# One ring of three PSUM banks for transposed scores and value product

## The chip, the cores and the metric

The kernel runs on one core of a Trainium2 chip. Its engines work side by side, each on its own queue in program order: TensorE (PE, with its weight loads shown apart as PEld), VectorE (DVE), ScalarE (ACT), GpSimd (POOL), and SyncE (SP), which issues the DMAs. They wait for each other through semaphores. TensorE writes its products to PSUM, which has eight banks of 128 partitions by 512 fp32 values; ScalarE and VectorE read them from there. The metric is the device time of one execution in microseconds, the median of several runs.

## The reference

Four layers in a row on a sequence of 2048 positions by 640 channels: attention, Fourier mixing, attention, Fourier mixing, each with a layer norm ahead and its input added behind.

```python
def _A_ref(x, wqkv, wo):                      # H = 32 heads of Dh = 20, window W = 256
    qkv = (x @ wqkv).reshape(B, S, 3, H, Dh).transpose(2, 0, 3, 1, 4)
    q, k, v = qkv[0], qkv[1], qkv[2]
    scores = jnp.einsum("bhqd,bhkd->bhqk", q, k) * (Dh ** -0.5)
    mask = (idx[:, None] - idx[None, :] >= 0) & (idx[:, None] - idx[None, :] < W)
    p = _softmax(jnp.where(mask[None, None], scores, -1e9), axis=-1)
    o = jnp.einsum("bhqk,bhkd->bhqd", p, v)
    return o.transpose(0, 2, 1, 3).reshape(B, S, D) @ wo
def _B_ref(x, ...):                            # y = Cr @ (x Wr^T) - Ci @ (x Wi^T)
x = x + _A_ref(_layernorm(x), A_wqkv, A_wo)
x = x + _B_ref(_layernorm(x), ...)             # and both once more
```

Only the two attention layers are touched by the change.

## The kernel before

An attention layer treats its 32 heads as eight quads of four, and the 2048 positions as 16 blocks of 128. The function `heads` walks through 8 x 16 = 128 steps, preceded by ten lead steps; one step is one quad and one block. Because of the window of 256, a block of queries sees at most three blocks of keys. In this document the steps of a layer are counted from 0 to 127, as the variable `t` does.

Every step does the same work for three places of the sequence at once:

- **Scores for the maximum** (`s_head`, line 553), ten steps ahead: queries by keys for one head, into the banks 2, 3 and 4 in turn. VectorE adds the mask and takes each row's maximum (line 558). Every fourth step `m_rows` transposes the maxima on TensorE (line 565), ScalarE copies them negated (line 567), and a DMA of SP puts them as an extra row under the queries (line 569).
- **Transposed scores** (`t_head`, line 578): keys by queries for one head, with that extra row, so that the maximum is already subtracted. ScalarE takes the exponential into SBUF (`t_exp`, line 587), and POOL clears what the mask excludes (`t_mask`, lines 593 and 597). The four heads of a quad are two halves `z` of two heads `e`; the text calls their transposed scores T00 and T01 (z = 0) and T10 and T11 (z = 1). Head `e` uses bank `e`: bank 0 for T00 and T10, bank 1 for T01 and T11.
- **Value product** (`pv`, line 608), one step behind: up to three blocks of keys, each as four matmuls on four column tiles of TensorE, which give one block of the output, 128 columns. A column of ones among the values gives the sum of the exponentials beside it. Bank 5 holds four such blocks side by side. After every second block ScalarE copies two of them, 256 columns, to the tile `ou` in SBUF (line 617); there are two such tiles in turn. After four blocks `finish` sends a tile out by two DMAs (lines 628 and 629), and ScalarE may write it again once these have landed.

Between the halves z = 0 and z = 1 of a step, `fill` puts other matmuls on TensorE: first the query and key projections of later quads (line 191, through banks 6 and 7), which come in rounds of 8, 8, 8 and 6 a step, and, when those are done (after step 91), the output projection. A finished projection is copied out by ScalarE (line 477), split on POOL and stored. Weights for it are split on ScalarE (line 160) and POOL (line 166).

The order on each engine is the order in which this Python code issues the instructions; no scheduler moves anything. A matmul into a bank waits for the engine that read the bank's former contents. Such a wait stops all of TensorE's later matmuls, though a weight load may run while an earlier matmul streams. The order inside one step is set by these lines:

```python
            for z in range(2):
                for e in range(2):
                    heads = [(t_head, t, e), (s_head, s, 1 - e)]
                    ...
                if 0 <= t < steps:
                    for e in range(2):
                        t_exp(t // 16, t % 16, z, e, e + 1)
                    ...
                if z:
                    relieve()
                    if 0 <= v < steps:
                        pv(v // 16, v % 16)
```

Of the kernel before, what the change touches and what calls it, by code (L numbers as in the profile page):

```python
# [11 lines left out]
AF = mybir.ActivationFunctionType  # L12
# [5 lines left out]
P = 128  # L18
# [45 lines left out]
class Net:  # L64
# [457 lines left out]
    def heads(self, xsrc, xdst, hook):  # L522
        nc = self.nc
        qp = [t.rearrange("p (z s) -> p z s", z=2) for t in self.qp]
        kp = [t.rearrange("p (z s) -> p z s", z=2) for t in self.kp]
# [4 lines left out]
        def defer(d, fn):  # L530
            later.setdefault(now[0] + d, []).append(fn)
# [3 lines left out]
        def load_v(n):  # L535
            if n < 4 * NQ:
                nc.sync.dma_start(self.vq[n % 3][:, :384].rearrange("p (t c) -> p t c", c=96),
                                  self.vd[n // 4][:, n % 4 * 4:n % 4 * 4 + 4, :])

        mc = {}  # L540
        turn = [0]

        def s_bank():
            turn[0] += 1
# [17 lines left out]
        def m_rows(quad, u):  # L562
            m = mc.pop((quad, u))
            p = self.banks[:16, s_bank(), :P]
            nc.tensor.transpose(p, m.rearrange("p z e j -> p (z e j)"), self.ident)  # L565
            mt = pool.tile([16, P], F32R, name="mt", tag="mt", bufs=1)
            nc.scalar.activation(mt, p, AF.Copy, scale=-1.0)
            for z in range(2):
                self.post(1, lambda z=z: nc.sync.dma_start(
                    qp[quad % 2][60:125:64, z, u * 512:(u + 1) * 512].bitcast(F32),  # L570
                    mt[8 * z:8 * z + 8, :].bitcast(F32)))

        pt = {}

        def t_head(quad, kb, z, e):
            n = min(NB - kb, 3)
            b = 64 * e
            nc.tensor.matmul(  # L578
                self.banks[:, e, :n * P], kp[quad % 2][b:b + 61, z, kb * P:(kb + 1) * P],
                qp[quad % 2][b:b + 61, z, kb * P:(kb + n) * P], start=True, stop=True)  # L580

        def t_exp(quad, kb, z, e0, e1):
            n = min(NB - kb, 3)
            if z + e0 == 0:
                i = 0 if (quad, kb) == (NQ - 1, NB - 1) else kb % 4
                pt[quad, kb] = self.pt[i].rearrange("p (h s) -> p h s", h=4)
            nc.scalar.activation(pt[quad, kb][:, 2 * z + e0:2 * z + e1, :n * P], self.banks[:, e0:e1, :n * P],  # L587
                                 AF.Exp, scale=SCALE)

        def t_mask(quad, kb, z):  # L590
            n = min(NB - kb, 3)
            t = pt[quad, kb][:, 2 * z:2 * z + 2, :]
            nc.gpsimd.affine_select(  # L593
                out=t[:, :, 0:P], in_=t[:, :, 0:P], pattern=[[0, 2], [1, P]],
                compare_op=OP.is_ge, fill=0.0, base=0, channel_multiplier=-1)
            if n == 3:
                nc.gpsimd.affine_select(  # L597
                    out=t[:, :, 256:384], in_=t[:, :, 256:384], pattern=[[0, 2], [-1, P]],
                    compare_op=OP.is_gt, fill=0.0, base=0, channel_multiplier=1)

        def pv(quad, qb):

            p = self.banks[:, 5, qb % 4 * P:qb % 4 * P + P]
            for kb in range(max(qb - 2, 0), qb + 1):
                t = pt[quad, kb]
                vq = self.vq[(4 * quad + kb // 4) % 3]
                for h in range(4):
                    nc.tensor.matmul(  # L608
                        p[32 * h:32 * h + 32, :], vq[:, 96 * (kb % 4) + 21 * h:96 * (kb % 4) + 21 * h + 32],
                        t[:, h, (qb - kb) * P:(qb - kb + 1) * P], start=kb == max(qb - 2, 0), stop=kb == qb,  # L610
                        tile_position=(0, 32 * h), skip_group_check=True)
            pt.pop((quad, qb - 2), None)
            if qb % 4 == 0:
                now_ou[0] = self.next("ou")
            if qb % 2:
                cs = slice(qb % 4 * P - P, qb % 4 * P + P)
                nc.scalar.activation(now_ou[0][:, cs], self.banks[:, 5, cs], AF.Copy)
            if qb % 4 == 3:
                finish(quad, qb // 4, now_ou[0])

        now_ou = [None]

        def finish(quad, bk, ou):
            sm = pool.tile([P, 16], F32, name="sm", tag="sm")
            rc = pool.tile([P, 16], F32, name="rc", tag="rc")
            cols = slice(bk * 512, (bk + 1) * 512)
            at = (2, 12, 14) if quad < NQ - 1 else (1, 5, 6)
            self.post(at[0], lambda: nc.sync.dma_start(sm, ou[0:P:32, :]))
            self.post(at[0], lambda: nc.sync.dma_start(
                self.od[4 * quad:4 * quad + 4, :, cols].rearrange("h r s -> (h r) s"), ou))  # L630
            self.post(at[1], lambda: nc.vector.reciprocal(out=rc, in_=sm))

            def store():
                nc.sync.dma_start(
                    self.rd[bk, 4 * quad:4 * quad + 4, :].rearrange("h (a b) -> (h a) b", b=16), rc)
                self.stored.add((quad, bk))
            self.post(at[2], store)
# [15 lines left out]
        def relieve():  # L653
            while self.heavy:
                self.relieve()
# [15 lines left out]
        def fill(n):  # L671

            k, size = 0, 1
            while k < size:
                r = more()
                if r == 0 and k == 0:
                    continue
                if r != 1:
                    return
                k += 1  # L680
                if k == 1:
                    left = self.left + 1
                    size = -(-left // max(1, round(left / n)))
            if self.left == 0:
                more()
                if self.heavy:
                    self.relieve()
# [4 lines left out]
        for step in range(-LEAD, steps + 1):  # L692
            now[0] = step
            self.wide, self.lead, self.tiled = step + LEAD > steps, step < -2, step < steps - 1
            for f in later.pop(step, []):
                f()
            s, t, v = step + LEAD, step, step - 1
            if due and s >= due[0][0]:
                while done[0] < due[0][1]:
                    fill(15)  # L700
                due.pop(0)
                q, j = (s + AHEAD) // 16, (s + AHEAD) % 16 // 4
                for i, f in enumerate(self.pack(q, j)):
                    defer(i // 3, f)
                for f in later.pop(step, []):
                    f()
            if v >= 0 and v % 4 == 3:
                load_v(v // 4 + 2)
            if done[0] < total:
                nf = max([FIRST if t < 0 else RATE]  # L710
                         + [(d - done[0]) / max(1, at - s) for at, d in due])
            elif made[0] < early:
                nf = LATE
            else:
                nf = LATE
            rows = ((s - 1) // 16, ((s - 1) % 16) // 4) if 4 <= s < steps + 4 and s % 4 == 0 else None
# [3 lines that stand above are left out]
                    for head, n, i in heads[::-1] if e else heads:  # L720
                        if 0 <= n < steps:
                            head(n // 16, n % 16, z, i)
                if 0 <= t < steps:
                    for e in range(2):
                        t_exp(t // 16, t % 16, z, e, e + 1)
                    t_mask(t // 16, t % 16, z)
                if z:
                    relieve()
                    if 0 <= v < steps:
                        pv(v // 16, v % 16)  # L730
                    if rows:
                        m_rows(*rows)
                if z == 0 and t >= 0 or t < -1 or t >= steps:
                    fill(nf)
                self.tick()
            if step > 16 * (NQ - 1):
                self.poll_late(step - 16 * (NQ - 1))
# [989 lines left out]
```

## Time and profile before

| what | value |
|---|---|
| median of 3 runs | 2180.93 us (2180.86 to 2181.6) |
| the profiled execution's own time | 2180.11 us |
| its span in the trace | 2178.4 us |
| line 578, transposed scores, x1024 | 310.6 us busy, mean 370 ns |
| line 587, exponentials, x1024 | 430.5 us busy, mean 470 ns |
| line 608, value product, x5760 | 214.9 us busy, mean 278 ns |
| line 553, scores for the maximum, x1024 | 280.2 us busy, mean 360 ns |
| line 191, filling projections, 512 columns, x1920 | 269.6 us busy, mean 394 ns |
| line 558, mask and maximum on VectorE, x1024 | 526.8 us busy, mean 558 ns |

Busy times of one line are unions, so overlapping matmuls count once; the mean is that of one instruction. The 128 steps of the first attention layer start at 161.1 us of the span, those of the second at 1242.6 us. In a row of a timeline stand the start, the length of a run of like instructions, the engine, the line, the operation, its tiles and shapes, and their count; in brackets the idle time ahead and what ended it. A matmul of TensorE is one row on PE and its weight load one on PEld.

### The profile page before, as it was taken

To read this page: it belongs to the slowest core of one execution; us is meant where nothing else is said; L and a number is where in the kernel's file an instruction comes from. 1 tells how busy PE (TensorE), PEld (TensorE's weight loads), DVE (VectorE), ACT (ScalarE), POOL (GpSimd) and SP (SyncE) were. 2 spreads that over 40 slices of the span, in tenths; PEclk is the share of its full clock that TensorE was granted. 3 is DMA by queue.
4 is the path that set the end of the run, shared out by engine and by line. 5 is a ranking of instruction groups with operands and counts; after the bars stand their busy time and mean duration, and the time that the engine had idled before them with its cause. 6 is when DMAs were issued, how large, how long until landed. Compare 5 with 4: busy or idle time off the path is not lost.

```text
span 2178.4 us, 49193 instructions
## 1 busy us (share of the span) xinstructions
PE 2123.0 (97%) x17893; PEld 1777.4 (82%) x17893; DVE 1615.0 (74%) x3933; ACT 1150.3 (53%) x2483; POOL 930.8 (43%) x1458
## 2 busy tenths in 40 slices
PE   7999999899999999999999999998999999999999
PEld 7987777687878888889999877776877788888899
DVE  6348788786897868777751578886868878687777
ACT  3117777766554545543431277776665545455522
POOL 3037777875514223230130477777754333331300
PEclk9999999999999999999999999999999999999999
DMA  5546666786435454657646466667753454546653
GB/s 184 176 154 189 202 183 213 219 221 212 134 119 175 138 185 129 216 192 264 218 135 190 152 200 185 201 203 219 226 188 134 131 187 137 164 148 217 219 175 126
DMA packets 221618, 395.40 MB, mean 182 GB/s; under 512 B 39360, under 2 KB 85952, under 8 KB 221376
## 3 DMA queue, kind: packets, MB, share of 16 engines
q1 hardware_dynamic: 221376, 392.26, 57.0%
q8 instruction: 141, 2.31, 0.5%
q14 instruction: 101, 0.83, 0.1%
HBM read 273.94 MB, written 117.05 MB: 179 GB/s over the span
## 4 chain that ended last, share of the span: by engine, by line
PE 81%; DVE 6%; POOL 5%; ACT 4%; issue 2%; DMA 2%; SPq 0%; ACTq 0%; DVEq 0%; POOLq 0%
PE banks L1266 27%; PE banks L173 14%; PE banks L191 13%; PE banks L608 8%; PE banks L578 6%; PE banks L1521 6%; PE banks L553 4%; POOL big L166 1%; POOL ou L1196 1%; DVE qp L166 1%; ACT big L928 1%; PE banks L273 1%; DVE pt L1197 1%; POOL rs L978 1%; PE banks L565 1%
## 5 line engine op out<-in xcount | busy, mean ns | idle before, releaser
L558 DVE CUSTOM_DVE_ANT_0 banks<-banks,mask 128x384 f32<-128x384 f32 (+2 forms) x1024 | 526.8, 558 | 157.9 <-PE banks L553 119.3
L587 ACT ACTIVATE pt<-banks 128x384 f32<-128x384 f32 (+2 forms) x1024 | 430.5, 470 | 179.3 <-PE banks L553 95.4
L578 PE MATMUL banks<-qp,kp 61*128 61x384 f32 (+2 forms) x1024 | 310.6, 370 | 14.5 <-DMA qp<-mt 7.8
L593 POOL TENSOR_SCALAR_AFFINE_SELECT pt<-pt 128x256 f32<-128x256 f32 x512 | 212.8, 416 | 183.5 <-ACT pt L587 133.2
L553 PE MATMUL banks<-kp,qp 60*128 60x384 f32 (+2 forms) x1024 | 280.2, 360 | 1.4 <-DVE mc L558 1.1
L191 PE MATMUL banks<-big,wc 64*128 64x512 f32 x1920 | 269.6, 394 | 0.4 <-DVE pt L374 0.4
L578 PEld LDWEIGHTS banks<-qp,kp 61*128 61x128 f32 x1024 | 175.2, 185 | 79.9 <-ACT pt L587 35.3
L608 PE MATMUL banks<-pt,vq 128*32 128x128 f32 x5760 | 214.9, 278 | 2.9 <-POOL pt L593 2.9
L191 PEld LDWEIGHTS banks<-big,wc 64*128 64x128 f32 x1920 | 183.0, 185 | 28.0 <-ACT x L477 5.2
L608 PEld LDWEIGHTS banks<-pt,vq 128*32 128x32 f32 x5760 | 144.0, 109 | 57.5 <-issue 51.5
L597 POOL TENSOR_SCALAR_AFFINE_SELECT pt<-pt 128x256 f32<-128x256 f32 x448 | 186.5, 416 | 0.0
L1196 POOL TENSOR_TENSOR pt<-pt,pt 128x512 f32<-128x512 f32 x36 | 61.0, 1695 | 291.0 <-DMA pt<-c 245.6
L553 PEld LDWEIGHTS banks<-kp,qp 60*128 60x128 f32 x1024 | 161.3, 186 | 20.3 <-DVE mc L558 10.3
L160 ACT ACTIVATE c<-pt 128x512 fp32r<-128x512 f32 x150 | 93.5, 626 | 150.2 <-POOL pt L1172 52.5
L160 ACT ACTIVATE qp<-pt 128x512 fp32r<-128x512 f32 (+1 forms) x195 | 119.8, 624 | 90.4 <-DVE pt L1197 38.3
L166 DVE TENSOR_TENSOR qp<-pt,qp 128x512 fp32r<-128x512 f32 (+1 forms) x195 | 153.7, 801 | 11.9 <-ACT qp L160 8.9
L166 DVE TENSOR_TENSOR c<-pt,c 128x512 fp32r<-128x512 f32 x150 | 123.4, 833 | 50.1 <-ACT c L160 48.4
L1266 PE MATMUL banks<-qp,big 128*128 128x512 f32 x630 | 151.1, 391 | 5.1 <-DVE qp L166 4.1
L558 DVE DVE_READ_ACCUMULATOR2_ANT mc<- 128x1 f32 x1024 | 145.2, 142 | 0.0
L1266 PEld LDWEIGHTS banks<-qp,big 128*128 128x128 f32 x630 | 117.0, 188 | 31.1 <-DVE qp L166 5.7
L1266 PE MATMUL banks<-qp,xc 128*128 128x512 f32 x480 | 117.9, 390 | 1.8 <-DVE xc L166 1.5
L1266 PEld LDWEIGHTS banks<-qp,xc 128*128 128x128 f32 x480 | 89.8, 188 | 22.2 <-DVE xc L166 2.3
(224 smaller groups left out, 4362.3 us busy)
## 6 DMA issues: line engine op xcount, KB each, us to landing
pt<-c SPq DMA_DIRECT2D x188, 512.0 KB
qk_d<-c SPq DMA_DIRECT2D x80, 512.0 KB
kp<-qk_d SPq DMA_DIRECT2D x384, 80.0 KB
qp<-qk_d SPq DMA_DIRECT2D x384, 80.0 KB
kp<-u_d SPq DMA_DIRECT2D x32, 640.0 KB
o_d<-ou SPq DMA_DIRECT2D x64, 256.0 KB
x_d<-x SPq DMA_DIRECT2D x48, 320.0 KB
v_d<-pt SPq DMA_DIRECT2D x16, 768.0 KB
```

What stands on the lines that cost most here:

```text
L160: nc.scalar.activation(hi, src, AF.Copy, scale=-1.0 if neg else 1.0)
L166: (eng or nc.vector).tensor_tensor(out=lo, in0=src, in1=hi.bitcast(F32), op=OP.subtract)
L173: self.nc.tensor.matmul(p, x, y, start=n == 0, stop=n == last)
L191: self.nc.tensor.matmul(ps[a], x[r], y[r], start=half + i == 0, stop=half == 1 and i == n - 1, skip_group_check=True)
L553: nc.tensor.matmul(p, qp[quad % 2][b:b + 60, z, qb * P:(qb + 1) * P], kp[quad % 2][b:b + 60, z, k0 * P:(qb + 1) * P], start=True, stop=True)
L558: nc.vector.tensor_tensor_reduce(out=p, in0=p, in1=self.mask[:, 384 - n * P:], scale=1.0, scalar=NEG, op0=OP.add, op1=OP.max, accum_out=mc ...
L578: nc.tensor.matmul(self.banks[:, e, :n * P], kp[quad % 2][b:b + 61, z, kb * P:(kb + 1) * P], qp[quad % 2][b:b + 61, z, kb * P:(kb + n) * P ...
L587: nc.scalar.activation(pt[quad, kb][:, 2 * z + e0:2 * z + e1, :n * P], self.banks[:, e0:e1, :n * P], AF.Exp, scale=SCALE)
L593: nc.gpsimd.affine_select(out=t[:, :, 0:P], in_=t[:, :, 0:P], pattern=[[0, 2], [1, P]], compare_op=OP.is_ge, fill=0.0, base=0, channel_mul ...
L597: nc.gpsimd.affine_select(out=t[:, :, 256:384], in_=t[:, :, 256:384], pattern=[[0, 2], [-1, P]], compare_op=OP.is_gt, fill=0.0, base=0, ch ...
L608: nc.tensor.matmul(p[32 * h:32 * h + 32, :], vq[:, 96 * (kb % 4) + 21 * h:96 * (kb % 4) + 21 * h + 32], t[:, h, (qb - kb) * P:(qb - kb + 1 ...
L1266: nc.tensor.matmul(self.banks[:, bk, :], p, b[q], start=start and m == 0, stop=stop and last and m == 2, skip_group_check=True)
```

## The change

The banks 0, 1 and 5 become one ring, through which the four transposed scores and the value product of every step go in the order in which they are issued. Five users a step go round three banks, so each gets the bank of the user three places ahead of it: T00 that of T10 of the step before, T01 that of T11, T10 that of the value product of the step before, T11 that of T00, the value product that of T01. A value product no longer has a quarter of a bank that others share, but the first 128 columns of its own, and so it is copied to `ou` in every step, 128 columns at a time.

```diff
-        turn = [0]
+        turn = [0, 0]
...
-        pt = {}
+        pt, tb = {}, {}
+
+        def t_bank():
+            turn[1] += 1
+            return (0, 1, 5)[turn[1] % 3]
 
         def t_head(quad, kb, z, e):
             n = min(NB - kb, 3)
             b = 64 * e
+            tb[e] = t_bank()
             nc.tensor.matmul(
-                self.banks[:, e, :n * P], kp[quad % 2][b:b + 61, z, kb * P:(kb + 1) * P],
+                self.banks[:, tb[e], :n * P], kp[quad % 2][b:b + 61, z, kb * P:(kb + 1) * P],
                 qp[quad % 2][b:b + 61, z, kb * P:(kb + n) * P], start=True, stop=True)
 
-        def t_exp(quad, kb, z, e0, e1):
+        def t_exp(quad, kb, z, e):
...
-            nc.scalar.activation(pt[quad, kb][:, 2 * z + e0:2 * z + e1, :n * P], self.banks[:, e0:e1, :n * P],
+            nc.scalar.activation(pt[quad, kb][:, 2 * z + e, :n * P], self.banks[:, tb[e], :n * P],
                                  AF.Exp, scale=SCALE)
...
-            p = self.banks[:, 5, qb % 4 * P:qb % 4 * P + P]
+            p = self.banks[:, t_bank(), :P]
...
-            if qb % 2:
-                cs = slice(qb % 4 * P - P, qb % 4 * P + P)
-                nc.scalar.activation(now_ou[0][:, cs], self.banks[:, 5, cs], AF.Copy)
+            nc.scalar.activation(now_ou[0][:, qb % 4 * P:qb % 4 * P + P], p, AF.Copy)
```

In the changed file the lines 578, 587, 608 and 617 are 583, 592, 613 and 620. On TensorE no matmul moves; what each waits for does. In step 55 of the first layer, from T10 to the value product, TensorE had in its queue (`qp`, `kp` are the packed queries and keys, `pt` the exponentials, `vq` the values):

```order
L578 MATMUL banks<-qp_104,kp_103 128x384 [waits Activation_49]
L553 MATMUL banks<-kp_560,qp_105 128x256
L553 MATMUL banks<-kp_560,qp_105 128x256 [waits DVE_49]
L578 MATMUL banks<-qp_104,kp_103 128x384 [waits Activation_49]
L608 MATMUL banks<-pt_94,vq_92 32x128 x4
L608 MATMUL banks<-pt_95,vq_92 32x128 x4
L608 MATMUL banks<-pt_96,vq_92 32x128 [waits Pool_49]
```

and now has

```order
L583 MATMUL banks<-qp_104,kp_103 128x384 [waits Activation_49]
L553 MATMUL banks<-kp_560,qp_105 128x256 [waits Activation_49]
L553 MATMUL banks<-kp_560,qp_105 128x256 [waits DVE_49]
L583 MATMUL banks<-qp_104,kp_103 128x384 [waits Activation_49]
L613 MATMUL banks<-pt_94,vq_92 32x128 [waits Activation_49]
L613 MATMUL banks<-pt_94,vq_92 32x128 x3
L613 MATMUL banks<-pt_95,vq_92 32x128 x4
L613 MATMUL banks<-pt_96,vq_92 32x128 [waits Pool_49]
```

The first matmul of the value product now waits for ScalarE too, and so does a score matmul behind a transposed maximum, whose wait stood on VectorE before.

On ScalarE, from the exponentials of T10 and T11 of that step to the first one of the next, there was

```order
L587 ACTIVATE pt_97<-banks 128x384 [waits PE_49,Pool_49]
L587 ACTIVATE pt_97<-banks 128x384 [waits PE_49]
L160 ACTIVATE wc<-x 128x256
L587 ACTIVATE pt_94<-banks 128x384 [waits PE_49,Pool_49]
L587 ACTIVATE pt_94<-banks 128x384 [waits PE_49]
```

and there is now

```order
L592 ACTIVATE pt_97<-banks 128x384 [waits PE_49,Pool_49]
L592 ACTIVATE pt_97<-banks 128x384 [waits PE_49]
L620 ACTIVATE ou_99<-banks 128x128 [waits PE_49]
L160 ACTIVATE wc<-x 128x256
L592 ACTIVATE pt_94<-banks 128x384 [waits PE_49,Pool_49]
```

A copy of a value product has come in, ahead of the split of a weight and of the next exponentials. The orders of VectorE, POOL and SP are unchanged.

More of the change, by code (lines that the diff above doesn't have):

```diff
@@ L577, in t_head @@
             b = 64 * e
+            tb[e] = t_bank()
             nc.tensor.matmul(
-                self.banks[:, e, :n * P], kp[quad % 2][b:b + 61, z, kb * P:(kb + 1) * P],
+                self.banks[:, tb[e], :n * P], kp[quad % 2][b:b + 61, z, kb * P:(kb + 1) * P],
                 qp[quad % 2][b:b + 61, z, kb * P:(kb + n) * P], start=True, stop=True)
-        def t_exp(quad, kb, z, e0, e1):
+        def t_exp(quad, kb, z, e):
             n = min(NB - kb, 3)
-            if z + e0 == 0:
+            if z + e == 0:
                 i = 0 if (quad, kb) == (NQ - 1, NB - 1) else kb % 4
                 pt[quad, kb] = self.pt[i].rearrange("p (h s) -> p h s", h=4)
-            nc.scalar.activation(pt[quad, kb][:, 2 * z + e0:2 * z + e1, :n * P], self.banks[:, e0:e1, :n * P],
+            nc.scalar.activation(pt[quad, kb][:, 2 * z + e, :n * P], self.banks[:, tb[e], :n * P],
                                  AF.Exp, scale=SCALE)
@@ L724, in heads @@
                     for e in range(2):
-                        t_exp(t // 16, t % 16, z, e, e + 1)
+                        t_exp(t // 16, t % 16, z, e)
                     t_mask(t // 16, t % 16, z)
```

## The prediction

> **What bounds the kernel now.** I read the page first, then the windows of the two stretches in which the edited lines run, then line L578 by itself, and last the timelines of single steps.
>
> ```profile
> PE 2123.0 (97%) x17893; PEld 1777.4 (82%) x17893; DVE 1615.0 (74%) x3933; ACT 1150.3 (53%) x2483; POOL 930.8 (43%) x1458
> PE 81%; DVE 6%; POOL 5%; ACT 4%; issue 2%; DMA 2%; SPq 0%; ACTq 0%; DVEq 0%; POOLq 0%
> 161.00:530.00 369.00, 360.43 (x5154) 276.92 (x5154) 285.65 (x1029) 268.18 (x664) 271.56 (x568) 0.99 0.68 203
> 1242.00:1606.00 364.00, 354.64 (x5085) 271.71 (x5089) 281.63 (x1022) 265.93 (x659) 271.69 (x567) 0.99 0.68 203
> ```
>
> (The two window rows give the stretch, its length, busy time and count of PE, PEld, DVE, ACT and POOL, the clock, and the DMA share.) TensorE is the bound: 97% busy, 81% of the chain. The 128 steps of an attention layer last 369 and 364 us. There TensorE is idle for 369.00 - 360.43 + 364.00 - 354.64 = 17.9 us in all; ScalarE is busy 73% of the time. A gain has to come out of those 17.9 us, or out of time that a pipelined matmul's row counts as busy while its weights wait.
>
> ```profile
> its engine sat idle before it (us, times) until:
>   ACT pt L587: 40.8, 143
>   issue: 28.8, 105
>   DMA qp<-mt: 7.8, 2
> L578 PE MATMUL banks<-qp,kp 61*128 61x384 f32 x896 | 279.5, 382 | 13.7 <-DMA qp<-mt 7.8 <-ACT pt L587 4.8
> L587 ACT ACTIVATE pt<-banks 128x128 f32<-128x128 f32 x64 | 16.3, 277 | 8.0 <-POOL pt L593 4.6 <-PE banks L578 2.0 <-PE banks L553 0.9
> L617 ACT ACTIVATE ou<-banks 128x256 f32<-128x256 f32 x128 | 49.4, 386 | 21.3 <-PE banks L608 15.0 <-DMA kp<-qk_d 0.5
> ```
>
> These are line L578 (loads and matmuls) and, of the groups by form, the transposed scores, the smallest exp and the copy of the value product. Loads of L578 wait for an exp 143 times, but loads run ahead of matmuls: of 40.8 us only 4.8 appear in front of full-size matmuls.
>
> A step issues on TensorE: scores T00, T01 (half z=0), then filling projections, then T10, T11 (z=1), then the value product PV, then the next T00. Before, T10 waits for the exp of T00 (bank 0) and T11 for that of T01 (bank 1). After, with five users in turn on three banks, each waits for the user three places back: T10 for the previous step's copy of PV, T11 for the exp of T00, PV for the exp of T01, the next T00 and T01 for the exps of T10 and T11 as now. So two waits move one place earlier and one new wait arises, at PV.
>
> **What the moved waits are worth, step by step.** Steps are counted 0 to 127 in a layer. Step 53 has eight filling matmuls, step 55 has six:
>
> ```profile
> 305.56 0.34 PE L578 MATMUL banks<-qp,kp 61*128 61x384 f32 x1
> 305.74 0.34 PE L578 MATMUL banks<-qp,kp 61*128 61x384 f32 x1
> 306.01 0.91 PE L608 MATMUL banks<-pt,vq 128*32 128x128 f32 x24
> 310.22 0.87 ACT L587 ACTIVATE pt<-banks 128x384 f32<-128x384 f32 x2
> 310.79 0.42 PE L578 MATMUL banks<-qp,kp 61*128 61x384 f32 x1
> 311.14 0.44 PE L578 MATMUL banks<-qp,kp 61*128 61x384 f32 x1
> 311.30 0.87 ACT L587 ACTIVATE pt<-banks 128x384 f32<-128x384 f32 x2 [0.21 <-PE banks L578]
> 311.51 0.86 PE L608 MATMUL banks<-pt,vq 128*32 128x128 f32 x24
> 312.31 0.44 PE L578 MATMUL banks<-qp,kp 61*128 61x384 f32 x1
> ```
>
> In step 53 (first three rows) T11 follows T10 by 0.18 us and PV follows T11 by 0.27: nothing waits. In step 55 the two exps end at 310.22 + 0.87 = 311.09; T11 starts 0.05 later, at 311.14, though 310.79 + 0.18 = 310.97 was its turn, and PV comes at 311.51. After the change T11 needs only the first exp of the pair, over by about 310.7 (310.22 and half of the pair's 0.87 with a little overlap), and starts at 310.97; PV needs the second exp, 311.14 at the earliest, and starts at 310.97 + 0.27 = 311.24. That is 0.27 us less for this step. The next T00 needs the exp of T10; T10 does not move, and that exp is the first of the pair at 311.30, so it ends near 311.8, ahead of T00's new turn at 312.31 - 0.27 = 312.04.
>
> *Term A.* The fill goes 8, 8, 8, 6, so every fourth of the first 92 steps has six: 23 in a layer. In five the score tile is short and the exp early; in twelve ScalarE also copies projections (term B); six are as step 55. Two layers: 12 x 0.27 = 3.2 us.
>
> *Term B.* In the twelve others (here step 43) ScalarE has no pause:
>
> ```profile
> 277.90 0.87 ACT L587 ACTIVATE pt<-banks 128x384 f32<-128x384 f32 x2
> 278.72 0.60 ACT L477 ACTIVATE x<-banks 128x512 f32<-128x512 f32 x1
> 279.22 0.87 ACT L587 ACTIVATE pt<-banks 128x384 f32<-128x384 f32 x2
> 279.96 0.62 ACT L477 ACTIVATE x<-banks 128x512 f32<-128x512 f32 x1
> 280.62 0.30 PEld L191 LDWEIGHTS banks<-big,wc 64*128 64x128 f32 x4 [0.16 <-ACT x L477]
> ```
>
> The next T01 still waits for the second pair's end at 280.09, and the next fill for the copy's end at 280.58. What PV gains is waited for there. Between 0 and 24 x 0.27 = 6.5 us; I take 0, since the last row shows that wait.
>
> *Term C.* Steps 92 to 97 have no fill, so T10 stands directly behind T01. The wait is seen in TensorE's row, and so is what follows it:
>
> ```profile
> 411.64 0.44 PE L578 MATMUL banks<-qp,kp 61*128 61x384 f32 x1 [0.44 <-ACT pt L587]
> 412.03 0.44 PE L578 MATMUL banks<-qp,kp 61*128 61x384 f32 x1
> 412.40 0.86 PE L608 MATMUL banks<-pt,vq 128*32 128x128 f32 x24
> 423.79 1.48 SPq L569 DMA_DIRECT2D qp<-mt  x2
> 429.56 0.65 PE L578 MATMUL banks<-qp,kp 61*128 61x384 f32 x1 [3.66 <-DMA qp<-mt]
> ```
>
> T11 could start at 411.64, where T10 starts now (it needs the same exp), so up to 412.03 - 411.64 = 0.39 a step, 12 x 0.39 = 4.7 us. But step 98 begins 3.66 us late, waiting for the DMA that carries the negated row maxima, which SP issues at 423.79 in a busy queue. Steps won ahead of it are waited for there, unless the queue moves up too. Between 0 and 4.7; I take 0.6, less than half of what steps 92 and 93 win (4 x 0.39 = 1.6), the two that lie ahead of the transpose which feeds that DMA.
>
> *Term D.* Late in the layer ScalarE is sometimes late for other reasons, as in step 124:
>
> ```profile
> 514.61 0.87 ACT L587 ACTIVATE pt<-banks 128x384 f32<-128x384 f32 x2
> 515.15 0.43 PE L578 MATMUL banks<-qp,kp 61*128 61x384 f32 x1
> 515.53 0.44 PE L578 MATMUL banks<-qp,kp 61*128 61x384 f32 x1
> 515.90 0.86 PE L608 MATMUL banks<-pt,vq 128*32 128x128 f32 x24
> ```
>
> T11 could start at 515.33, PV then at 515.60: 0.30 less. I find four such places in both layers together, of 0.2 to 0.3, and a dozen steps in which T11 is about 0.05 late: 1.5 us, between 0 and 2.
>
> *Term E, the copies.* 128 copies of 256 columns become 256 of 128. The nearest row is the exp of a 128 x 128 tile, 277 ns, against 386: 256 x 0.277 - 49.4 = 21.5 us more ScalarE work. What hides it is the time from PV's end to the end of the next T00 matmul:
>
> ```profile
> 312.06 0.42 ACT L160 ACTIVATE wc<-x 128x256 fp32r<-128x256 f32 x1
> 312.85 0.87 ACT L587 ACTIVATE pt<-banks 128x384 f32<-128x384 f32 x2 [0.37 <-PE banks L578]
> 314.14 0.86 PE L608 MATMUL banks<-pt,vq 128*32 128x128 f32 x24
> 315.07 0.39 ACT L617 ACTIVATE ou<-banks 128x256 f32<-128x256 f32 x1
> ```
>
> The old copy starts at 315.07, and the exps of step 57 would start 0.54 after that step's T00, at 315.47. A copy of 0.28 in the same place ends at 315.35, in time. Where ScalarE is busy then (the projection copies, the split L160, which now queues behind the copy), the exps come up to 0.28 late; that is the price if cover fails. But the exps of step 56 end at 313.72 and PV at 314.14 is their first user on this path: 0.37 us of slack behind 0.05 of signalling. So 0 on TensorE; the upper bound is the 24 steps after projection copies and 12 after a split, 36 x 0.28 = 10.1 us. Below nothing it can't go: the odd copies get shorter, but no one waits for them.
>
> A page of the Trainium skill speaks against this edit: Perfetto Trace Analysis, section Optimizing Scalar/DVE Operations, says that grouping into larger operations helps a saturated engine, and gives ScalarE about 51 ns of data-access overhead per PSUM instruction (twice that in profiled latency). By that figure 128 more instructions would be an estimated 6.5 to 13 us of ScalarE time. No row here has a 128-column copy, and at 73% ScalarE is not saturated in these stretches, so by the page's own condition the sum stands.
>
> What else moves: PV of a block's first step is now copied at once instead of one step later, so that copy waits for the DMAs that emptied the same buffer two blocks earlier, one step sooner. The tightest place:
>
> ```profile
> 475.94 0.51 SPq L629 DMA_DIRECT2D o_d<-ou  x1
> 482.06 0.44 PE L578 MATMUL banks<-qp,kp 61*128 61x384 f32 x1
> ```
>
> The store is issued at 475.94 and the first copy would come at about 482.06: 6.1 us. The slow DMA quoted above took at most 429.56 - 423.79 = 5.8 us, so no wait; 0, and above nothing only if a landing takes longer. No DMA, no POOL instruction and nothing on VectorE is added; VectorE's four score reductions have their own ring of banks. Queued behind PV on TensorE are only the next T00 and the m transposes, behind the copy on ScalarE the m copy and the next exps.
>
> **Sum.** 3.2 + 0 + 0.6 + 1.5 + 0 = 5.3 us less. The profiled execution took 2180.11 us, which becomes 2174.8; it lies 0.8 below the median 2180.93 (runs 2180.86 to 2181.6), which becomes 2175.6.
>
> **Rivals.**
> - *More.* Term C comes whole, since the chain that leads to the m DMA begins at steps that also get shorter, and a little of B: 4.1 + 0.5 more, 2171. For it: 0.39 us a step is in TensorE's own row. Against it: the 3.66 us wait.
> - *Absorbed.* VectorE, POOL or a DMA wait later gives back much of A too; less than 4.4 us is left, 2179. For it: 286 of 369 us of VectorE and 272 of POOL are busy, and a step made 0.27 shorter has less room. Against it: in step 55 both have pauses.
> - *Slower: ScalarE becomes late.* Place: the exps of T00 and T01 behind a PV copy that is itself behind a projection copy or ahead of a split; price 0.28 each. It decides once the lateness passes the 0.37 us of slack at PV, which needs the copy and another late piece together. With all of the 36 places paid and the gains kept: 2180.9 - 5.3 + 10.1 = 2185.7; where a late exp also delays POOL's mask and so a later PV, 2187.
> - *Slower: the copy waits for the store.* It starts where a landing takes over 6.1 us. At 2 us a place and three places a layer, 12 us: 2188.
> - *The wait at PV merely replaces that at T11* (the change would do nothing): PV needs an exp that ends 0.10 us before its new start in step 55; a little later exp leaves A smaller. This is counted under absorbed.
>
> **How the numbers follow.** Forecast (2175.6) 0.35, more 0.15, absorbed 0.32, ScalarE late 0.13, store 0.05. A measurement of this kernel can tell about 0.2%, 4.4 us, from no change. Forecast and more are faster by that: 0.50; absorbed is within it: 0.32; the last two are slower: 0.18. The range runs from 2169 (terms B and C partly beyond "more") to 2185, which leaves out the last rivals' far ends. The likeliest case's own range is 2173 to 2177.
>
> **What would show it.** Right: steps like 55 last 2.36 instead of 2.63 us, T11 follows T10 by 0.18 there, step 98 waits longer than 3.66 us for the m DMA, the copy line has 256 instructions near 0.28, ScalarE's busy time is about 20 us up, and the two stretches are 2 to 3 us shorter each. Wrong: PV's loads wait for the exp, exps of T00 start later than 0.54 after their matmul in many steps, or copies wait for DMAs.

## The result, and the profile after

The changed kernel takes 2174.83 us (median of 9 runs, 2170.36 to 2177.61) against 2181.5 us for the kernel before on the same chip (9 runs, 2178.74 to 2183.06): a ratio of 0.997, 95% interval 0.9961 to 0.9979. Run again later beside other kernels it took 2174.3 us, a ratio of 0.997, interval 0.9958 to 0.9981. The prediction said 2175.6. Further down, one run of one kernel (one copy a step) took 6054.21 us where its ten others lie at 2181.1 to 2184.48; it is left out there.

The page of the changed kernel answers to the two page rows shown before: engines, and the chain that ended last.

```profile
PE 2116.4 (97%) x17893; PEld 1768.5 (81%) x17893; DVE 1611.6 (74%) x3933; ACT 1167.9 (54%) x2611; POOL 932.6 (43%) x1458
PE 81%; DVE 6%; POOL 4%; ACT 4%; DMA 3%; issue 2%; SPq 0%; ACTq 0%; POOLq 0%; DVEq 0%
```

ScalarE has 128 instructions and 17.6 us more, TensorE 6.6 us less, with the same number of instructions. The windows of the two attention stretches, cut at the same distance from their first and last steps as before:

```profile
161.72:526.11 364.39, 356.79 (x5154) 271.93 (x5154) 284.47 (x1029) 277.05 (x728) 271.31 (x568) 1.00 0.68 206
1237.87:1599.99 362.12, 351.60 (x5086) 267.36 (x5090) 280.36 (x1022) 274.50 (x722) 271.38 (x567) 0.99 0.68 204
```

They last 4.6 and 1.9 us less (369.00 and 364.00 before); ScalarE is busy 9 us longer in each. What lies outside them moved by less than 0.8 us a piece. TensorE's idle time in them is 18.1 us, as it was (17.9): the time came out of rows that counted as busy (the large matmuls of the transposed scores: 279.5 us before, 271.8 now), where a pipelined matmul stood behind weights that were not yet loaded.

Line L578, the transposed scores, is L583 in the changed kernel. What ended the idle time before its loads and matmuls:

```profile
  issue: 27.4, 99
  ACT pt L592: 22.4, 99
  DMA qp<-mt: 7.7, 2
  ACT ou L620: 2.1, 8
```

Its large matmuls and the copy, of the groups by form (busy time and mean ns of one, then the idle time before):

```profile
L583 PE MATMUL banks<-qp,kp 61*128 61x384 f32 x896 | 271.8, 376 | 9.7 <-DMA qp<-mt 7.7 <-ACT ou L620 0.4 <-ACT pt L592 0.3
L620 ACT ACTIVATE ou<-banks 128x128 f32<-128x128 f32 x256 | 72.0, 281 | 36.3 <-PE banks L613 27.8
```

Loads wait for an exp 22.4 us instead of 40.8, and for the new copy (L620) only 2.1 us in 8 places. In front of the large matmuls the exp has all but gone (0.3 us instead of 4.8); the DMA of the row maxima is as it was (7.7 instead of 7.8).

Step 55 of the first layer, the prediction's example, in the timeline of the changed kernel:

```profile
309.97 0.34 PE L583 MATMUL banks<-qp,kp 61*128 61x384 f32 x1
310.09 0.34 PE L583 MATMUL banks<-qp,kp 61*128 61x384 f32 x1
310.36 0.86 PE L613 MATMUL banks<-pt,vq 128*32 128x128 f32 x24
311.15 0.44 PE L583 MATMUL banks<-qp,kp 61*128 61x384 f32 x1
310.36 0.59 PEld L613 LDWEIGHTS banks<-pt,vq 128*32 128x32 f32 x24 [0.19 <-ACT pt L592]
311.29 0.28 ACT L620 ACTIVATE ou<-banks 128x128 f32<-128x128 f32 x1
```

T11 (310.09) follows T10 (309.97) by 0.12 us instead of 0.35, PV comes at 310.36 and the next T00 at 311.15. The step, which starts at 308.88, lasts 2.28 us instead of 2.63. The fifth row shows the new wait: PV's first load stands 0.19 us for the exp of T01. It costs nothing here, since PV follows T11 by 0.27, which is what it took in step 53 before without any wait.

Summed over the first 92 steps of a layer, by the place of the step in a block of 16 (trace before against trace after, first and second layer):

| steps | change, us |
|---|---|
| first 92 steps together | -2.87, -2.76 |
| place 7 (six steps a layer, as step 55) | -2.12, -2.11 |
| place 6 | -0.53, -0.46 |
| places 11 and 12 | -1.30 and +1.06, -1.34 and +1.10 |
| places 3 and 4 | -0.29 and +0.29, -0.30 and +0.30 |
| steps 92 to 96 | 0.00, +0.03 |
| steps 97 and 98 | -2.03, -0.53 |
| steps 99 to 126 | +0.29, +1.37 |

In a second profiled execution of the changed kernel the first 92 steps win 2.92 and 2.96 us, and from step 92 on nothing is left: -0.22 and +0.98 in all. So the change is worth its gain in the first 92 steps of each layer, 5.6 to 5.9 us in the two layers together, and what the trace shows behind them moves from one execution to the next. (The rows of places leave out pairs such as 0 and 1, where -0.56 and +0.48 nearly cancel.)

### The profile page after: what moved, and what is told of

The parts are those of the page before. It is cut to its first block, busy times and chain, and to the rows that moved or that the text cites. A ratio compares the mean times of both kernels' runs of the same rounds, so it can differ in the third digit from the quotient of the medians.

```text
span 2171.9 us, 49261 instructions
## 1 busy us (share of the span) xinstructions
PE 2116.4 (97%) x17893; PEld 1768.5 (81%) x17893; DVE 1611.6 (74%) x3933; ACT 1167.9 (54%) x2611; POOL 932.6 (43%) x1458
## 4 chain that ended last, share of the span: by engine, by line
PE 81%; DVE 6%; POOL 4%; ACT 4%; DMA 3%; issue 2%; SPq 0%; ACTq 0%; POOLq 0%; DVEq 0%
PE banks L1269 27%; PE banks L173 14%; PE banks L191 13%; PE banks L613 8%; PE banks L1524 6%; PE banks L583 6%; PE banks L553 4%; POOL ou L1199 1%; POOL big L166 1%; DVE qp L166 1%; ACT big L931 1%; PE banks L273 1%; PE banks L565 1%; POOL rs L981 1%; ACT big L160 1%
## 5 line engine op out<-in xcount | busy, mean ns | idle before, releaser
L583 PE MATMUL banks<-qp,kp 61*128 61x384 f32 (+2 forms) x1024 | 302.8, 365 | 9.7 <-DMA qp<-mt 7.7
L583 PEld LDWEIGHTS banks<-qp,kp 61*128 61x128 f32 x1024 | 176.8, 185 | 68.0 <-issue 27.4
L553 PEld LDWEIGHTS banks<-kp,qp 60*128 60x128 f32 x1024 | 163.7, 185 | 26.7 <-DVE mc L558 16.3
```

Of the source, the lines that this page charges most:

```text
L553: nc.tensor.matmul(p, qp[quad % 2][b:b + 60, z, qb * P:(qb + 1) * P], kp[quad % 2][b:b + 60, z, k0 * P:(qb + 1) * P], start=True, stop=True)
L583: nc.tensor.matmul(self.banks[:, tb[e], :n * P], kp[quad % 2][b:b + 61, z, kb * P:(kb + 1) * P], qp[quad % 2][b:b + 61, z, kb * P:(kb + n) ...
```

## The experiments

The theory: the gain is T11's wait for the exp of T01 moving one place back to PV, in the steps with short filling; the smaller copies cost nothing on TensorE as long as T11 no longer needs the second exp; what steps 92 to 97 could win is lost in the wait for the row maxima at step 98. The rivals: T10's earlier freedom is what helps; the copies cost, and would cost more; or the gain is something else in the order of work.

**One copy a step, banks as before.** The kernel before, with only the copies changed:

```
-            if qb % 2:
-                cs = slice(qb % 4 * P - P, qb % 4 * P + P)
-                nc.scalar.activation(now_ou[0][:, cs], self.banks[:, 5, cs], AF.Copy)
+            cs = slice(qb % 4 * P, qb % 4 * P + P)
+            nc.scalar.activation(now_ou[0][:, cs], self.banks[:, 5, cs], AF.Copy)
```

> The kernel before with one edit: the value product is copied out in every step, 128 columns at a time; banks as before. If the gain comes from the ring (my theory), the copies alone bring nothing: 2181.5 us, 0 to 1.5 more than before, with steps like 55 still at 2.62 us and T11 still 0.05 us behind the second exp. If the smaller copies bring it, some 2176. If the copies make ScalarE late on the path, 2184 to 2188.

It took 2182.46 us (2181.1 to 2184.48), a ratio of 1.0011, interval 1.0002 to 1.002: some 2.4 us more than before, beyond the 0 to 1.5 expected. The first 92 steps are 1.31 and 1.37 us longer than before, of which 0.94 and 0.73 lie in place 8 of the block, and 0.35 in place 6. Step 55 is as before, 2.63. The trace of this kernel in two steps of place 8, step 56, which starts at 312.61, and step 88, which starts at 400.84:

```profile
312.75 0.28 ACT L616 ACTIVATE ou<-banks 128x128 f32<-128x128 f32 x1 [0.27 <-PE banks L608]
312.92 0.41 ACT L160 ACTIVATE wc<-x 128x256 fp32r<-128x256 f32 x1
313.23 0.87 ACT L587 ACTIVATE pt<-banks 128x384 f32<-128x384 f32 x2
314.00 0.34 PE L578 MATMUL banks<-qp,kp 61*128 61x384 f32 x1
314.18 0.40 PE L578 MATMUL banks<-qp,kp 61*128 61x384 f32 x1
```

```profile
401.15 0.73 ACT L160 ACTIVATE big<-we 128x640 fp32r<-128x640 f32 x1
401.78 0.86 ACT L587 ACTIVATE pt<-banks 128x384 f32<-128x384 f32 x2
402.32 0.44 PE L578 MATMUL banks<-qp,kp 61*128 61x384 f32 x1
402.70 0.44 PE L578 MATMUL banks<-qp,kp 61*128 61x384 f32 x1
```

In step 56 the new copy stands ahead of the split of line 160, so the exps come 0.62 us behind T00 instead of 0.54 and end at 314.10. T11 needs the second one: its row starts on its turn, 0.18 behind T10, but its weights load 0.07 us later than before (1.54 behind T00 instead of 1.46), so the row is 0.40 long instead of 0.33, and the step lasts 2.69 us instead of 2.62. In step 88 the split is longer, the exps come 0.94 behind T00 instead of 0.54, T10 and T11 both wait for them, and the step lasts 3.02 instead of 2.62. In the changed kernel both steps have the exps just as late (0.62 and 0.94) and last 2.62 and 2.65, because there T11 needs the first exp only and T10 none of this step. So the copies are not free by themselves; it is the ring that hides them.

**Which of the ring's moved waits pays.** Two kernels, each with all the changed copies, in which three users go round two banks and the other two keep a bank of their own. In the first T11 keeps its old wait:

```
-            return (0, 1, 5)[turn[1] % 3]
+            return (0, 5)[turn[1] % 2]
...
-            tb[e] = t_bank()
+            tb[e] = 1 if e else t_bank()
```

> The changed kernel, but T01 and T11 share bank 1 as before, and only T00, T10 and the value product go round banks 0 and 5. T10 then waits for the copy of the value product as in the change, T11 for the exp of T01 as before. If the wait of T11 is what the change shortens (my theory), the gain is gone: 2180 to 2182.5, steps like 55 back at 2.62 us. If the freed T10 brings the gain, 2175 and 2.28 us.

2181.88 us (2178.11 to 2184.94), a ratio of 1.0009, interval 1.0 to 1.0018. T10 and T11 of step 55, which starts at 306.81:

```profile
307.91 0.34 PE L583 MATMUL banks<-qp,kp 61*128 61x384 f32 x1
308.27 0.44 PE L583 MATMUL banks<-qp,kp 61*128 61x384 f32 x1
308.27 0.18 PEld L583 LDWEIGHTS banks<-qp,kp 61*128 61x128 f32 x1 [0.17 <-ACT pt L592]
```

T11's load waits for the exp of T01 as before. Step 55 lasts 2.63 us, and the first 92 steps are 1.18 and 0.96 us longer than before, almost as with the copies alone. T10 freed by itself brings nothing.

In the second T10 keeps its old wait:

```
-            return (0, 1, 5)[turn[1] % 3]
+            return (1, 5)[turn[1] % 2]
...
-            tb[e] = t_bank()
+            tb[e] = t_bank() if e else 0
```

> The mirror image: T00 and T10 share bank 0 as before, and T01, T11 and the value product go round banks 1 and 5. T10 waits for the exp of T00 as before, T11 for the copy of the value product. By my theory nearly the whole gain stays: 2174 to 2177, steps like 55 at 2.28 to 2.32 us, since T10's own wait ends there at about its turn. If the freed T10 brings the gain, 2180 to 2182.

2177.15 us (2174.36 to 2178.74), a ratio of 0.9985, interval 0.9976 to 0.9994. Step 55 in its trace, from 308.19 on:

```profile
309.30 0.55 PE L583 MATMUL banks<-qp,kp 61*128 61x384 f32 x2
309.77 0.86 PE L613 MATMUL banks<-pt,vq 128*32 128x128 f32 x24
310.56 0.44 PE L583 MATMUL banks<-qp,kp 61*128 61x384 f32 x1
```

The step lasts 2.37 us, 0.26 less than before: the prediction's 0.27, and not the 2.28 to 2.32 that I expected of this kernel. The first 92 steps win 2.06 and 1.99 us, the six steps like 55 have 1.56 of it. The remaining 0.09 us a step of the full ring need T10 as well: its weights load 0.87 us behind T00 there, 1.08 before, so that T11's load comes sooner too and T11 follows T10 by 0.12 and not by the 0.18 of an undisturbed pair before.

**Every copy made twice.** The changed kernel, with the copy instruction issued a second time (the same result is written again):

```
             nc.scalar.activation(now_ou[0][:, qb % 4 * P:qb % 4 * P + P], p, AF.Copy)
+            nc.scalar.activation(now_ou[0][:, qb % 4 * P:qb % 4 * P + P], p, AF.Copy)
```

> The changed kernel with each copy of a value product done twice: 256 x 0.278 = 71 us more work on ScalarE. If the copies lie under the T00 matmul with about 0.12 us to spare (my theory), the second copy shifts the exps by up to 0.28 us: the twelve six-matmul steps lose up to 0.25 each at the value product, and the 24 steps after projection copies up to 0.28 each: 3 to 10 us more than the change, 2178 to 2185. If ScalarE has room in every step: 0 to 1 more, 2175 to 2176. If its work adds up one for one: 2246.

2176.47 us (2175.3 to 2180.16), a ratio of 0.9985, interval 0.9976 to 0.9994. By its own row (256 more instructions, 71.1 us) ScalarE has more than three times the work that the change added, and against the changed kernel that costs 1.6 us by the medians of the two groups of runs, 3.3 by their ratios: no more than the low end of what I expected. The first 92 steps still win 2.42 and 2.25 us. With the ring the cover is wide: in step 56 the exps come 0.93 us behind T00 here, and the step lasts 2.64 us.

```profile
L621 ACT ACTIVATE ou<-banks 128x128 f32<-128x128 f32 x256 | 71.1, 278 | 8.1
```

**The load of the row maxima moved ahead on SP's queue.** In the changed kernel step 98 waits 2.87 us for it in the first layer:

```profile
421.91 1.81 SPq L569 DMA_DIRECT2D qp<-mt  x2
426.35 0.66 PE L583 MATMUL banks<-qp,kp 61*128 61x384 f32 x1 [2.87 <-DMA qp<-mt]
```

The edit issues three loads of the next part's input, which stand on the same queue, three steps later:

```
-                    self.defer(i, lambda i=i: self.load_y([i]))
+                    self.defer(i + 3, lambda i=i: self.load_y([i]))
```

> The changed kernel, with loads 1 to 3 of the next block input issued three steps later each, so that the load of the mask that step 98 waits for stands ahead of them on SP's queue. Theory that the gain of the steps from 92 on is swallowed by the wait at step 98 (2.87 us in layer 1 of the changed kernel, 7.7 us in both layers) because that load is issued late: it is issued 1 to 2 us earlier, the two waits together fall from 7.7 to 4 to 6 us, and the kernel takes 1 to 4 us less than the changed one, 2171 to 2174 us, a ratio of 0.995 to 0.997. Rival, that the wait is bound by the transfer and the other loads beside it, or that the later loads are themselves waited for: the same as the changed kernel within 1 us, or slower.

2171.57 us (2169.78 to 2174.44), a ratio of 0.9958, interval 0.9947 to 0.997. Its trace:

```profile
420.85 1.22 SPq L569 DMA_DIRECT2D qp<-mt  x2
436.21 1.29 SPq L569 DMA_DIRECT2D qp<-mt  x2
439.99 0.41 PE L583 MATMUL banks<-qp,kp 61*128 61x384 f32 x1 [1.75 <-DMA qp<-mt]
```

Step 97 starts at 422.05 here and at 421.50 in the changed kernel, so against the steps the load (that of the row maxima; the expectation calls it the mask) is issued 1.6 us sooner (422.05 - 420.85 is 1.20 ahead, 421.91 - 421.50 is 0.41 behind). In this trace the wait for it at step 98 is gone in both layers, step 97 lasts 3.41 us instead of 4.86 in the first and 2.88 instead of 6.81 in the second. But the next load of the same kind, four steps on, is now waited for: 1.75 us at 439.99, and step 101, which that wait ends, lasts 4.84 us instead of 3.01. It and the changed kernel were then run once more, on one chip:

> The kernel with the three loads issued later once more, so that it stands on one chip beside the changed kernel. Theory that it saves about 2 us on the changed kernel because the two waits for the mask at step 98 shrink: a ratio 0.0005 to 0.0015 below that of the changed kernel. Rival, that its lower time was the chip's: within 0.0003 of it.

> The changed kernel once more, beside the three that are built on it: a ratio of 0.9965 to 0.9985 to the kernel before, about 2175 us, as measured.

2172.99 us (2171.37 to 2175.84), a ratio of 0.9964, interval 0.9951 to 0.9976, beside 0.997 for the changed kernel. TensorE waited for the row maxima 7.0 us in three places there (one of them step 98 of the second layer, 1.80), and 8.7 us in two in the changed kernel. Both times it came out faster than the changed kernel beside which or after which it ran, by 1.3 us in this pair and 3.3 between the two groups of runs, but the intervals overlap, so whether it is faster stays unsure. The place of that load in the queue moves the wait: issued 1.4 to 3.3 us sooner against the steps, it is not waited for at step 98 in three of the four layers of the two traces. Whether it also lands sooner because fewer transfers run beside it was not tried apart. Of the 4.8 to 5.6 us that steps 97 and 98 are shorter than before the change, steps 101 and 102 give back 3.3 to 4.2 in three of these layers and 0.8 in the fourth (the second layer of the first trace).

**The copy issued behind the projection copies.** In late steps such as 124 the copy now stands ahead of two splits of line 160, and the exps behind them:

```profile
509.89 0.28 ACT L620 ACTIVATE ou<-banks 128x128 f32<-128x128 f32 x1
510.06 1.14 ACT L160 ACTIVATE kp<-cr 128x512 fp32r<-128x512 f32 x2
511.10 1.62 ACT L592 ACTIVATE pt<-banks 128x384 f32<-128x384 f32 x4
511.36 0.33 PE L583 MATMUL banks<-qp,kp 61*128 61x384 f32 x1
511.64 0.43 PE L583 MATMUL banks<-qp,kp 61*128 61x384 f32 x1
512.02 0.86 PE L613 MATMUL banks<-pt,vq 128*32 128x128 f32 x24
```

The first exp starts at 511.10, 1.35 us behind the step's T00 at 509.75; before the change it was 1.07 (514.61 behind 513.54). The edit makes `pv` return its copy, which the loop calls after the step's posted work:

```
                 if z:
                     relieve()
-                    if 0 <= v < steps:
-                        pv(v // 16, v % 16)
+                    copy = pv(v // 16, v % 16) if 0 <= v < steps else None
+                    if rows and copy:
+                        copy()
+                        copy = None
...
                 self.tick()
+                if z and copy:
+                    copy()
```

> The changed kernel, with the copy of a value product issued behind the projection copies posted for the step instead of ahead of them (not in the steps with mask rows). Theory that in the late steps such as step 124 the new copy stands ahead of the two splits of line 160 and makes the first exponential late (1.35 us behind T00 there, 1.06 before the change): it is back at about 1.06, step 124 takes 2.85 instead of 3.06 us, and the kernel 0.3 to 0.8 us less than the changed one; in the steps with one copy only little moves. Rival, that these steps are held by something else (the second exponential, or POOL): step 124 stays at 3.0 to 3.1 us, no change of the time; or a loss of up to 1 us, where the copy, now later, is what the next T11 or T00 waits for.

2182.64 us (2176.56 to 2189.1), a ratio of 1.0006, interval 0.9997 to 1.0016: the whole gain of the change is gone. Step 124 did what was expected in kind (2.95 us instead of 3.06, the exp 1.22 behind T00), but the stretches behind the two attentions (from the start of step 127 to the next layer's step 0, and to the end of the span) grew from 720.1 to 724.2 us and from 573.8 to 579.4. The windows of the 20 us in which the first attention ends, of the changed kernel and of this one:

```profile
518.30:538.30 20.00, 17.81 (x159) 15.54 (x156) 16.65 (x45) 10.56 (x23) 5.37 (x9) 1.00 0.75 241
```

```profile
519.00:539.00 20.00, 16.19 (x138) 14.71 (x136) 13.39 (x36) 7.39 (x17) 3.33 (x7) 0.83 0.52 170
```

TensorE issues 138 matmuls instead of 159, at a granted clock of 0.83 instead of 1.00. What it waits for there, in the waits of this kernel and, below, of the changed one:

```profile
PE banks L173 <- DVE x L977: 4.2, 2, 3.8
DVE cr L789 <- DMA rr<-r_d: 3.8, 3, 2.5
```

```profile
PE banks L173 <- DVE x L970: 2.2, 5, 0.6
```

The last value products' copies stand behind the splits; the reciprocals of the sums, which go through memory (`rr<-r_d`), land later, VectorE waits for them, and TensorE behind the attention for VectorE. To see whether that is all, the copy was put first again from step 125 on (the test above becomes `(rows or t >= 125) and copy`):

> The changed kernel with the copy issued last in the steps before step 125 only; from step 125 on it stands first, as in the changed kernel. Theory that the copy-last kernel lost its time at the end of the attention alone, where the last copies stood behind the splits, the stores of the last value product came later and TensorE waited and was then granted a lower clock (0.83 in the first 20 us behind the attention): the stretches behind the two attentions are back at 720.1 and 573.8 us (724.2 and 579.4 with the copy last everywhere), step 124 stays at 2.95 us, and the kernel takes 0.3 to 1.0 us less than the changed one. Rival, that the copy's place in the other steps is what loses: it stays near 2182 us.

2178.13 us (2175.43 to 2183.79), a ratio of 0.9986, interval 0.9977 to 0.9994. About half came back: 722.4 and 575.8 us behind the attentions, a granted clock of 0.91 and 1.00 in the 20 us behind the start of step 127 (0.83 and 0.88 without the guard). In the traces what is left of the loss lies there: from the start of the last transposed score to that of the hundredth matmul behind it the changed kernel takes 11.9 us in both layers, this one 13.9 and 13.6, the one without the guard 15.7 and 17.2, and the 900 matmuls behind that take 204 to 205 us in all three. (This trace is of a run of 2175.44 us, at the fast end of this kernel's range, so it doesn't show all of the 3.8 us between the medians.) Step 124 itself copies the last product of the next to last group of four, whose store and sums also come later; that this is the other half was not tried.

**Both edits together**, first with the copy last everywhere, then with the guard:

> Both edits together, as a candidate. If each does what the theory says, their gains add: 1.3 to 4.8 us less than the changed kernel, 2170 to 2173.5 us. If neither does, the same as the changed kernel, a ratio of 0.9965 to 0.9985 to the kernel before.

2181.79 us (2177.41 to 2187.63), a ratio of 1.0003, interval 0.9993 to 1.0012.

> The three later loads and the guarded copy together, as a candidate: if both theories hold, 1.5 to 3.5 us less than the changed kernel, a ratio of 0.995 to 0.997 to the kernel before. If neither does, that of the changed kernel.

2176.95 us (2173.47 to 2179.12), a ratio of 0.9983, interval 0.9973 to 0.9992. Neither beats the changed kernel: what the copy's place wins in one step of a layer it loses at the layer's end. The later loads alone have the lowest medians measured.

## Why the prediction was right, point by point

- **The sum.** 5.3 us less were forecast, and the medians fell by 6.7 (2181.5 - 2174.83). Part of that agreement is luck. In the first trace, both layers together, A gave 1.0 us more than forecast and B 0.5 (places 11 and 12); C gave 0.6 less, and behind step 98 only some 0.2 of D's 1.5 can be seen; place 6, where T11 also waited for the second exp, gave 1.0. Those may be the dozen steps that D counts at 0.05 each; it doesn't say which they are.
- **Term A, right in mechanism, too small.** Each of the twelve steps like 55 wins 0.35 us, not 0.27: 4.2 us for 3.2. The step that failed is "T10 does not move". Its matmul doesn't, but its load does (0.87 us behind T00 instead of 1.08), and T11 follows closer. The kernel with T10's old bank shows the 0.27 by itself (0.26).
- **Term B, right.** What places 3 and 11 win is given back one step later, in full in places 3 and 4, and but for 0.24 in 11 and 12. Step 43 went from 2.62 to 2.40 us and step 44 from 2.91 to 3.13.
- **Term C, nothing instead of 0.6, and for another reason than the one given.** I had the gain of steps 92 to 96 made there and lost at step 98. It is not made: together they last as long as before, in both executions. In these steps T11 is let go sooner, and stands behind the scores of the other ring and POOL's mask instead:

```profile
412.20 0.44 PE L553 MATMUL banks<-kp,qp 60*128 60x384 f32 x1 [0.28 <-DVE mc L558]
413.86 0.41 PE L613 MATMUL banks<-pt,vq 128*32 128x128 f32 x4 [0.44 <-POOL pt L598]
```

 The first is a matmul of the scores in step 93, the second PV's third block there, both in the timeline of the changed kernel. In its groups:

```profile
L553 PEld LDWEIGHTS banks<-kp,qp 60*128 60x128 f32 x1024 | 163.7, 185 | 26.7 <-DVE mc L558 16.3
```

 and before the change:

```profile
L553 PEld LDWEIGHTS banks<-kp,qp 60*128 60x128 f32 x1024 | 161.3, 186 | 20.3 <-DVE mc L558 10.3
```

 The scores' loads wait 16.3 us for VectorE in all, where it was 10.3. "Step 98 waits longer than 3.66" came out wrong in the first profile of the changed kernel (2.87) and right in the second (3.92), and the second layer's wait went from 4.15 to about 4.8 in both: a wait at the end of a queue that moves from one execution to the next is no good test.
- **Term D, mostly wrong.** Step 124 was to last 0.30 us less; it lasts 0.09 less in the first layer (3.15 to 3.06) and 0.07 more in the second (3.07 to 3.14). The splits of line 160 stand behind the new copy, and the exp that T11 waits for comes 0.28 later, the length of the copy. That is the rival "ScalarE becomes late", at its predicted price of 0.28. In the term it was left out. Behind step 98 only step 117 is clearly shorter in both layers of both profiles, by 0.10.
- **Term E, right, but its reason held only half.** In the first 92 steps the copies cost nothing on the path that can be seen; the kernel with the copies alone, though, loses 1.3 us a layer there. The prediction's slack was measured at PV; with the old banks T11 is the user that has none, and in step 88 T10 as well. ScalarE's rows of this copy grew by 72.0 - 49.4 = 22.6 us (21.5 forecast), its busy time by 17.6. Two copies of 128 columns take 2 x 281 - 386 = 176 ns more than one of 256. The page Perfetto Trace Analysis of the Trainium skill, section Optimizing Scalar/DVE Operations, gives ScalarE about 51 ns of data-access overhead a PSUM instruction and about twice that in profiled latency; taken as the whole cost of one more instruction, as in the prediction's estimate of 6.5 to 13 us, that is too low, against 22.6 us by the rows here. Its condition, that grouping can help if the engine is saturated, agrees with the twice-made copies, which cost so little on an engine that is not.
- **The store behind `ou`: right.** No row of the copy names the DMA of the store as what it waited for.
- **The signs.** Step 55 lasts 2.28 us, not 2.36, and the copy line is as forecast. Two signs of being wrong came up, though, and in the first 92 steps they cost next to nothing: the exps come 0.6 us or more behind T00 in 26 and 27 of a layer's 128 steps (11 and 11 before), and PV's loads wait for an exp in 39 places, 7.9 us in all. At 0.20 us each these are no longer than the gaps that PV's loads had before without a wait (250 times, 51.5 us). As signs they were badly chosen.
- **The rivals.** What "absorbed" describes is seen in the steps from 92 on, and with the later loads at step 102; the steps up to 91 keep their gain. "More" fell with term C.

## What to carry to other kernels

A ring of three banks with five users does not take waits away; it moves each to the user that stands three places on, so look for the user that has slack and let the wait fall there. Smaller, earlier copies on an engine that is not the bound are cheap only if the next user in line does not need the instruction queued behind them; ask that of each user, not of the engine. When a step that feeds a queued transfer gets shorter, look up the next transfer of the same kind before booking the gain.

## What was not expected

- Two freed waits, of which one is worth nothing alone (T10: 2.63 us a step, as before) and the other 0.26, are worth 0.35 together.
- Where the work behind an attention came 1.7 to 5.4 us late, TensorE's granted clock was mostly lower too: in the 20 us behind the start of step 127 it was 0.83 and 0.88 (first and second layer) with the copy last, 0.91 and 1.00 with the guard, and 1.00 in the changed kernel. The second layer with the guard lost its 1.7 us (13.6 against 11.9 to the hundredth matmul) at a clock of 1.00, so the clock isn't needed for such a loss; what part it has in the others, and whether the idle time lowered it, wasn't tried apart.
- Where a step waits for a transfer, two profiled executions of the changed kernel differ by 1 us (step 97 of the first layer: 4.86 and 5.91), as much as several of the prediction's terms; the steps that wait for no transfer agree within 0.1 us in sum over a layer's six steps like 55.
